# 64-row products in pairs, folds in two buffers and two parts, and rows 0 and 8 in halves, in a fused spectral and token-mixing kernel

## The chip, the cores and the metric

The kernel runs on 1 core of one Trainium2 chip. The metric is the device time in microseconds (us), the median of the runs shown. TensorE (PE) multiplies, VectorE (DVE) and ScalarE (ACT) work elementwise, SyncE (SP) issues nearly all DMAs; GpSimd (POOL) only sets four constants.

## The reference

x has 2048 rows (s) of 512 columns (d). Two branches are mixed by a gate that each row has:

```
g = sigmoid(sum_d(x * gate_w))
a = irfft2( rfft2(x) * (w_r + 1j * w_i) )             # over s (2048) and d (512)
h = layernorm(x) over d
u = gelu( h[s,d] * w1[s,f] summed over s + b1 )       # f: 1792
b = ( u[d,f] * w2[f,s] summed over f + b2 ), transposed to [s,d]
out = g * a + (1 - g) * b
```

Inputs and output are bfloat16; the normalisation has no weights.

## The kernel before

All of x is kept in SBUF. Its rows are taken as s = 512 q + 4 p + r: partition p (128), block q and residue r (4 each); row group j = 4q + r, 16 in all.

**The mixer** is two plain products on PE. The first (`m1`, L711 to L717) runs over the 14 column tiles `ft` of w1 and adds up 16 row groups in a bank of PSUM: product (ft, j) has 128 rows and 512 columns of the normalised x (`h`). Row groups are taken in the order 0, 8, 4, 12, and then residue by residue; for the first seven tiles each row group is multiplied for all seven before the next, so PE can begin as soon as group 0 is normalised. Gelu is on ACT (L732). The second (`m2`, L1022 to L1031) runs over the 16 row groups, with 14 products of 512 columns each in a bank; ACT evicts (L1034), DVE for the last two groups (L1041), of which the last is cut into 256, 128 and 128 columns.

**Normalisation.** DVE has a mean and variance (L489, L490; row 8 in two halves of 256, L505 and L507), ACT takes the root (L521), DVE the reciprocal (L526), and then DVE (L531, row groups 0, 8, 4, 1 and 12) or ACT (L537) writes `h`. Ahead of the first product PE multiplies ten times by a constant (L361).

**The spectral branch** is a transform over s in steps (radix 4 across q and r on DVE, dense products within), one over d (L664), the multiplication by the filter (L830 to L860), and then the inverse: radix 4 (L596 to L612), and the dense inverse products over s (L885 to L946). These are taken for each residue r (0 to 3), for each parity h of the columns and for lt = 0 and 1, the even and the odd wavenumbers. For odd r (`rs` = 1) the product at L903 has 128 rows of wavenumbers and 256 columns of a table; at lt = 0 the table holds a cosine (or sine) and the same with the sign turned for the upper 64 partitions, so that both s and its mirror come out. ACT evicts it to `zz` (L918); for even r it evicts to `ze` (L923), and DVE forms sum and difference (L933 to L937). DVE then adds lt = 0 and lt = 1 into z (`fq`, L943 and L944). The inverse over d (`i3`, L986 to L990) is taken for pairs of row groups p = 0 to 7, ACT evicts it with the gate (L994), and a fold on DVE (`es`, L1009 to L1013) forms the full row: a copy of two edge columns (L1009), a sum and a difference into the buffer `es`, and a sum and a difference back. L1047 adds the mixer's part, and SP stores.

**What sets the order.** Every step is a task with an engine, an estimated duration, what it reads and writes, a priority, and the buffers that it takes (`alloc`) and gives back (`free`). A planner (`Plan.order`, L173) runs these through a simulated clock and emits each engine's instructions in the order in which they were started. Each engine then runs its own list in that order; on PE the `m1` and `m2` products (late priority) are placed wherever no spectral product is ready. PSUM banks: four `acc`, two `fa`, two `fb`. The buffer `es` is there once (NES, L297).

Of the kernel before, what the change touches and what calls it, by code (L numbers as in the profile page):

```python
# [12 lines left out]
Alu = mybir.AluOpType  # L13
# [3 lines left out]
P = 128  # L17
# [227 lines left out]
def tt(n):  # L245
    return 0.07 + n / 1920.0
# [6 lines left out]
def d1(n):  # L253
    return 0.07 + n / 960.0
# [6 lines left out]
def mm(*ns):  # L261
    return sum(max(n, 62) / 2400.0 + 0.0025 for n in ns)
# [3 lines left out]
def tiny(k):  # L266
    return 0.09 * k + 0.06
# [3 lines left out]
def kernel(  # L271
# [22 lines left out]

    pool = ctx.enter_context(tc.tile_pool(name="sb", bufs=1))
    psum = ctx.enter_context(tc.tile_pool(name="ps", bufs=1, space=bass.MemoryType.PSUM))
    NES = 1  # L297

    def sb(shape, dt, tag, bufs=1):
        return pool.tile(shape, dt, tag=tag, name=tag, bufs=bufs)  # L300

    def ps(shape, dt, tag, bufs):
        return psum.tile(shape, dt, tag=tag, name=tag, bufs=bufs)
# [53 lines left out]
    def warm():  # L357
        pw = ps([P, D], F32, "fa", 2)
        zero = nc.const_aps.tensor(0.0, [P, 1], F32).bitcast(BF16)
        for _ in range(NWARM):  # L360
            T.matmul(pw[:], lhsT=zero[:, 0:1].to_broadcast([P, P]), rhs=zero[:, 0:1].to_broadcast([P, D]), start=True, stop=True)  # L361
# [107 lines left out]
    HACT = set(range(NJ)) - {0, 8, 4, 1, 12}  # L469
    PQ0 = -0.5  # L470
    ASTAT = {12, 4, 1}
    sqs = []
    rect = {}
    for r in range(4):
        xk = [("x", r, q) for q in range(4)]
        groups = [[q] for q in Q0] if r == 0 else [[0], [1], [2, 3]] if r == 1 else [[0, 1], [2], [3]] if 12 + r in ASTAT else [[0, 1], [2, 3]]
        t["xf", r] = None
        for b, qs in enumerate(groups):
# [8 lines left out]
            for j in js:  # L487
                def bn(j=j):
                    V.bn_stats(out=t["stats"][:, j, :], in_=t["x"][:, j // 4, j % 4, :])  # L489
                    V.bn_aggr(out=t["mv"][:, j, :], in_=t["stats"][:, j, :])  # L490
                def sum1(j=j):
                    xj, junk = t["x"][:, j // 4, j % 4, :], t["h"][:, j // 4, j % 4, :]
                    A.activation(junk, xj, ActF.Copy, scale=-1.0 / D, accum_out=t["mv"][:, j, 0:1])

                def sum2(j=j):
                    xj, junk = t["x"][:, j // 4, j % 4, :], t["h"][:, j // 4, j % 4, :]
                    A.activation(junk, xj, ActF.Square, bias=t["mv"][:, j, 0:1], scale=1.0, accum_out=t["mv"][:, j, 1:2])
                if j in ASTAT:
# [26 lines left out]
            def rec(colv=colv, mvv=mvv, js=js, here=here):  # L525
                V.reciprocal(colv("rstd"), colv("rstd"))  # L526
                if any(j in HACT for j in js):
                    V.scalar_tensor_tensor(colv("nmr"), mvv(0), 1.0 if here else -1.0, colv("rstd"), op0=Alu.mult, op1=Alu.mult)  # L528
                for j in js:
                    if j not in HACT:  # L530
                        V.tensor_scalar(t["h"][:, j // 4, j % 4, :], t["x"][:, j // 4, j % 4, :], t["mv"][:, j, 0:1],  # L531
                                        t["rstd"][:, j:j + 1], op0=Alu.add if j in ASTAT else Alu.subtract, op1=Alu.mult)
            own = [j for j in js if j not in HACT]
            rect[g] = add("DVE", 0.17 + 0.08 * (len(own) < len(js)) + 0.35 * len(own), rec, reads=xb + mvk, writes=[("rstd", *g)] + [("h", j) for j in own], prio=1.2 * r - (0.2 if r else 0.9))
# [170 lines left out]
    def w1of(ft):  # L705
        return sum(ft >= b for b in WB[1:3])
# [1 line left out]
    def bankof(ft):  # L708
        return "fa" if ft == 0 else "fb" if ft in (5, 6) else "acc"

    def m1(ft, j):  # L711
        if j == jorder[0]:
# [3 lines left out]
        T.matmul(t["u", ft][:], lhsT=w[:, j // 4, j % 4, c * P:(c + 1) * P],  # L716
                 rhs=t["h"][:, j // 4, j % 4, :], start=(j == jorder[0]), stop=(j == jorder[-1]))  # L717

    order = [(ft, j) for c in range(6) for j in jorder[2 * c:2 * c + 2] for ft in range(NF)]
    order += [(ft, j) for ft in range(NF) for j in jorder[12:]]  # L720
    order += [(ft, j) for ft in range(NF, NFT) for j in jorder]
# [4 lines left out]
    for n, (ft, j) in enumerate(order):  # L726
        last = j == jorder[-1]
        bank = bankof(ft)
        m1t.append(add("PE", mm(512), lambda ft=ft, j=j: m1(ft, j), reads=[("w1", w1of(ft), j), ("h", j)] + ([("w1", 0, j, n) for n in range(2)] if j % 4 == 0 else []), writes=[("u", ft)],
                       prio=10 + n * 1e-3, alloc=[bank] if j == jorder[0] else (), free={NF - 1: ["wa"], NF + 3: ["wb"], NFT - 1: ["wb"]}.get(ft, ()) if last else ()))  # L730
# [144 lines left out]
    for lt in range(2):  # L875
# [5 lines left out]
        if lt == 0:  # L881
            add("SP", 0.5, lambda: dma(t["B"][0:1, 0].rearrange("p e (c v) l -> p (e c) (v l)", c=2), t["s8"][P - 8:P]),
                reads=["s8"], writes=[("T", 0, 0), ("T", 0, 1)], prio=0, nbytes=8192)

    i1t = {}  # L885
    for rs, h in ((0, 0), (0, 1), (1, 0), (1, 1)):
        for r in (rs, rs + 2):
            for lt in range(2):
                tag = ("fa", "fb")[lt]

                def i1(h=h, r=r, lt=lt, tag=tag):
                    if "zz" not in t:
                        t["zz"] = sb([P, 2, 2, 2, 2, 2, 2, P], BF16, "X")
                        t["ze"] = sb([P, 2, 2, 2, 2, L], BF16, "h")
                    p1 = t["i1", h, r, lt] = ps([P, 2, L], F32, tag, 2)
                    o, w = ti_at(r)
                    ti = t["ti"][:, o:o + w]
                    for v in range(2):
                        d = lambda c: t["B"][:, lt, r, 2 * c + v, h:L:2]
                        if r % 2:  # L900
                            for c in range(2):
                                f = (2 * c if lt == 0 else 5 - c) * P
                                T.matmul(p1[:, v], lhsT=d(c), rhs=ti[:, f:f + L], start=(c == 0), stop=(c == 1))  # L903
                        else:
                            u = ti[:, 256 * lt:256 * lt + 256]
# [68 lines left out]
    for p in range(NJ // 2):  # L974
# [23 lines left out]
        def tb2j(j0=j0):  # L998
            tbuf(j0)
            return t["tb_"][:, j0:j0 + 3:2]  # L1000

        def es(p=p, j0=j0, late=late, tb2j=tb2j):
            e, s = eo_v(p), sb([P, 2, 2, 2, P], BF16, "es", NES)
            o = tb2j() if late else e
            if late:
                for i in range(2):
                    V.tensor_scalar_add(e[:, i, 0, 0:129], e[:, i, 0, 0:129], t["ombb2"][:, j0 + 2 * i:j0 + 2 * i + 1])
            o = o.rearrange("p j h (k d) -> p j (h k) d", k=2)
            V.tensor_copy(s[:, :, :, :, 0], e[:, :, :, 0:129:128].rearrange("p j h k -> p j k h"))  # L1009
            V.tensor_add(s[:, :, 0, :, 1:P], e[:, :, :, 1:P], e[:, :, :, P + 1:L])  # L1010
            V.tensor_sub(s[:, :, 1, :, P - 1:0:-1], e[:, :, :, 1:P], e[:, :, :, P + 1:L])
            V.tensor_add(o[:, :, 0:4:3], s[:, :, :, 0], s[:, :, :, 1])
            V.tensor_sub(o[:, :, 2:0:-1], s[:, :, :, 0], s[:, :, :, 1])  # L1013
        add("DVE", 0.2 + tiny(1) + 4 * tt(512) + (0.3 if late else 0), es, reads=(k1 + ["omg"]) if late else [],
            writes=ko if late else k1, prio=4, alloc=["es"], free=["es"], after=gates if late else ())

        for i, j in enumerate((j0, j1)):
            n = 2 * p + i
# [77 lines left out]
```

## Time and profile before

| | us |
|---|---|
| median of 3 runs | 126.31 (126.26 to 126.35) |
| the profiled execution | 126.59 |
| its span, first to last instruction | 124.8 |
| PE busy in the span | 121.2 |
| DVE busy | 113.4 |
| ACT busy | 82.6 |

The prediction quotes the profile of one execution. "Busy" is time in which an engine worked. The chain of work that ended last is followed back from the last instruction, at each step to what released it. A timeline row has a start, a length, an engine, a line, and what was written from what; in brackets stands idle time ahead of it and what ended that. L12 is line 12 of the kernel. A row of groups has the count behind an x, then the busy time, and the mean length of one in ns. Matmuls are pipelined: a row's length is from a product's start to the end of its last column, so neighbours overlap.

### The profile page before, as it was taken

How to read it: one execution, taken by the hardware profiler on the slowest of the kernel's cores; microseconds unless marked ns; L12 is line 12 of the kernel's file. 1: busy time of each engine (PE TensorE's matmuls, PEld its weight loads, DVE VectorE, ACT ScalarE, POOL GpSimd, SP SyncE). 2: the span in 40 equal slices, each digit the busy share in tenths (PEclk: the TensorE clock that was granted, in tenths of full speed). 3: DMA queues.
4: the chain of work that ended last, by engine and by line, in shares of the span. 5: the costliest groups of instructions: out<-in, count | busy, mean ns of one | idle time of the engine just before them, and what ended most of it. 6: DMA issues, size and time to landing. Idle time of an engine off the chain costs nothing.

```text
span 124.8 us, 2188 instructions
## 1 busy us (share of the span) xinstructions
PE 121.2 (97%) x773; PEld 68.8 (55%) x773; DVE 113.4 (91%) x274; ACT 82.6 (66%) x169; POOL 0.2 (0%) x4
## 2 busy tenths in 40 slices
PE   7999999999999999999999999999999999999990
PEld 2345655555655466744455555555578767655590
DVE  1889999999989999999999999999979999999961
ACT  3795889699999999999520003742289999952200
POOL 0000000000000000000000000000000000000000
PEclk9999999999999999999999999999999999999999
DMA  4998999994649936799999900000000000011751
GB/s 122 347 302 277 397 395 389 375 294 86 145 87 302 266 74 156 226 411 414 417 420 415 377 17 0 0 5 0 3 0 0 0 5 0 0 63 45 318 205 47
DMA packets 18202, 23.09 MB, mean 185 GB/s; under 512 B 2174, under 2 KB 15888, under 8 KB 18192
## 3 DMA queue, kind: packets, MB, share of 16 engines
q1 hardware_dynamic: 17616, 22.34, 52.6%
q10 hardware_dynamic: 576, 0.62, 1.6%
q8 instruction: 6, 0.10, 0.3%
q14 instruction: 4, 0.03, 0.1%
HBM read 20.84 MB, written 2.10 MB: 184 GB/s over the span
## 4 chain that ended last, share of the span: by engine, by line
PE 97%; DVE 0%; issue 0%
PE acc L1028 33%; PE acc L716 31%; PE fb L716 6%; PE fb L1028 5%; PE fa L361 4%; PE fa L716 3%; PE fa L664 1%; PE fb L664 1%; PE fa L903 1%; PE fa L566 1%; PE fb L903 1%; PE fa L565 1%; PE fb L990 1%; PE fa L990 1%; PE fa L568 1%; PE fa L567 1%
## 5 line engine op out<-in xcount | busy, mean ns | idle before, releaser
L716 PE MATMUL acc<-h,wb 128*128 128x512 bf16 x112 | 27.0, 379 | 0.0
L1028 PE MATMUL acc<-gl,wb 128*128 128x512 bf16 (+1 forms) x98 | 24.5, 372 | 0.0
L1028 PE MATMUL acc<-gl,wa 128*128 128x512 bf16 (+1 forms) x98 | 23.8, 372 | 0.0
L1034 ACT ACTIVATE x<-acc,ombb,omg 128x512 bf16<-128x512 f32 x12 | 9.1, 782 | 20.8 <-PE acc L1028 20.8
L1028 PEld LDWEIGHTS <-wa 128*128 128x128 bf16 x126 | 13.4, 113 | 9.9
L1028 PEld LDWEIGHTS <-wb 128*128 128x128 bf16 x126 | 13.3, 114 | 9.2
L716 PE MATMUL acc<-h,wa 128*128 128x512 bf16 x64 | 17.4, 385 | 0.0
L716 PEld LDWEIGHTS <-wb 128*128 128x128 bf16 x112 | 10.7, 98 | 10.3
L716 PEld LDWEIGHTS <-wa 128*128 128x128 bf16 x112 | 10.4, 99 | 10.5 <-issue 0.7
L571 ACT CAST xp<-fa 128x512 bf16<-128x512 f32 x16 | 9.1, 584 | 2.4 <-PE fa L568 2.3
L746 ACT ACTIVATE x<-x 128x512 bf16<-128x512 bf16 x16 | 10.0, 649 | 0.0
L716 PE MATMUL fb<-h,wa 128*128 128x512 bf16 x32 | 9.9, 379 | 0.0
L489 DVE BATCH_NORM_STATS2 stats<-x 128x6 f32<-128x512 bf16 x12 | 8.1, 676 | 1.9 <-DMA x<-in_A_x_dram 1.9
L732 ACT ACTIVATE gl<-acc,b1f 128x512 bf16<-128x512 f32 x11 | 7.7, 701 | 2.8 <-PE acc L716 2.8
L537 ACT ACTIVATE h<-x,nmr,rstd 128x512 bf16<-128x512 bf16 x11 | 8.4, 808 | 1.1 <-DVE nmr L528 1.1
L716 PE MATMUL fa<-h,wa 128*128 128x512 bf16 x16 | 6.3, 392 | 0.0
L664 PEld LDWEIGHTS <-X 128*128 128x128 bf16 x64 | 4.7, 98 | 2.2
L994 ACT ACTIVATE B<-fa,g 128x512 bf16<-128x512 f32 x8 | 5.8, 727 | 0.0
L994 ACT ACTIVATE B<-fb,g 128x512 bf16<-128x512 f32 x8 | 5.8, 719 | 0.0
L361 PE MATMUL fa<-const-float32-0.0 128*128 128x512 bf16 x10 | 4.4, 629 | 0.8 <-PEq L1080 0.8
L671 ACT CAST X<-fb 128x512 bf16<-128x512 f32 x8 | 5.1, 638 | 0.0
L671 ACT CAST X<-fa 128x512 bf16<-128x512 f32 x8 | 5.1, 634 | 0.0
(176 smaller groups left out, 235.9 us busy)
## 6 DMA issues: line engine op xcount, KB each, us to landing
wb<-in_B_w_dram SPq DMA_DIRECT2D x11, 512.0 KB
wa<-in_B_w_dram SPq DMA_DIRECT2D x7, 512.0 KB
wa<-in_B_w_dram SPq DMA_DIRECT2D x2, 896.0 KB
wb<-in_B_w_dram SPq DMA_DIRECT2D x4, 384.0 KB
out_dram<-x SPq DMA_DIRECT2D x3, 512.0 KB
x<-in_A_x_dram SPq DMA_DIRECT2D x2, 512.0 KB
wa<-in_B_w_dram SPq DMA_DIRECT2D x4, 224.0 KB
rot<-dft_ti SPq DMA_DIRECT2D x1, 768.0 KB
```

Source lines behind the costliest of these rows:

```text
L361: T.matmul(pw[:], lhsT=zero[:, 0:1].to_broadcast([P, P]), rhs=zero[:, 0:1].to_broadcast([P, D]), start=True, stop=True)
L489: V.bn_stats(out=t["stats"][:, j, :], in_=t["x"][:, j // 4, j % 4, :])
L537: add("ACT", 0.71, lambda j=j: A.activation(t["h"][:, j // 4, j % 4, :], t["x"][:, j // 4, j % 4, :], ActF.Identity, bias=t["nmr"][:, j:j ...
L571: add("ACT", act(512), lambda r=r, dq=dq: A.copy(xe(r)[:, :, :, dq, :], t["pa", r, dq][:]), reads=[("pa", r, dq)], writes=[("X", r, dq)], ...
L664: T.matmul(pb[:, k % 2, k // 2], lhsT=t["X"][:, lt, EX[e], c, k, :], rhs=tbl(k, c), start=True, stop=True)
L671: A.copy(t["X"][:, lt, EX[e]].rearrange("p c j l -> p (c j l)").rearrange("p (h c g b) -> p h c g b", h=2, c=2, b=2)[:, :, c], t["pb", lt, ...
L716: T.matmul(t["u", ft][:], lhsT=w[:, j // 4, j % 4, c * P:(c + 1) * P], rhs=t["h"][:, j // 4, j % 4, :], start=(j == jorder[0]), stop=(j == ...
L732: gelus.append(add("ACT", act(512, 1) , lambda ft=ft: A.activation(t["gl"][:, ft, :], t["u", ft][:], ActF.Gelu_apprx_tanh, bias=t["b1f"][: ...
L746: A.activation(t["x"][:, q, r, :], t["x"][:, q, r, :], ActF.Copy, accum_out=t["glog"][:, 4 * q + r:4 * q + r + 1])
L994: A.activation(eo_v(p)[:, n].rearrange("p h (n w) -> p h n w", w=2), t["i3", j][:].rearrange("p h (w n) -> p h n w", w=2), ActF.Copy, scal ...
L1028: T.matmul(t["y", j, m][:, cs], lhsT=w[:, o, 512 * q + r:512 * q + 512:4], rhs=t["gl"][:, ft, cs], start=(ft == 0), stop=(ft == NFT - 1))
L1034: A.activation(tbuf(j).rearrange("p h d -> p (h d)"), t["y", j, 0][:], ActF.Identity, bias=t["ombb2"][:, j:j + 1], scale=t["omg"][:, j:j + 1])
```

## The change

1. **Odd residues, lt = 0.** For each h one task `i1s` takes the place of two `i1` tasks (r = 1 and 3). It makes products of 64 rows and 128 columns: the lower 64 partitions into a bank `fa`, the upper 64 into a bank `fb`, each adding c = 0 and 1, for two residues and two v: 16 products per h. The table's sign-turned copy isn't read any more: ACT copies the two banks to a new tile `zo` (in the buffer `h`, behind `ze`), and DVE forms their sum and difference into `zz` (`eo2`).
2. **The banks of lt = 1** for odd r: `fa` for r = 1 and `fb` for r = 3 (all `fb` before).
3. **Folds.** `es` has two buffers. The fold is two tasks, `es` and `es2`, the second with the earlier priority (3.95, against 4). For seven of eight folds ACT copies the edge (`ese`), not DVE.
4. **Rows 0 and 8.** `nrm` normalises 256 columns; the second half is a task of its own. The products of these rows in the first seven tiles are of 256 columns each, all seven tiles with the first half, then all seven with the second. For row 8 the aggregation of the statistics is its own task.
5. **Warm-up.** Nine products of 512 columns and one of 256, in place of ten of 512.

```diff
-    NES = 1
+    NES = 2
...
-        for _ in range(NWARM):
-            T.matmul(pw[:], lhsT=zero[:, 0:1].to_broadcast([P, P]), rhs=zero[:, 0:1].to_broadcast([P, D]), start=True, stop=True)
-    NWARM = 10
-    add("PE", 0.42 * NWARM, warm, writes=["warmed"], prio=-5, alloc=["fa"], free=["fa"])
+        for n in [D] * 9 + [L]:
+            T.matmul(pw[:, 0:n], lhsT=zero[:, 0:1].to_broadcast([P, P]), rhs=zero[:, 0:1].to_broadcast([P, n]), start=True, stop=True)
+    add("PE", 4.0, warm, writes=["warmed"], prio=-5, alloc=["fa"], free=["fa"])
...
+    HALF = (0, 8)
...
+    def nrm(j, n):
+        c = slice(L * n, L * n + L)
+        V.tensor_scalar(t["h"][:, j // 4, j % 4, c], t["x"][:, j // 4, j % 4, c], t["mv"][:, j, 0:1], t["rstd"][:, j:j + 1], op0=Alu.subtract, op1=Alu.mult)
...
-                            if n:
-                                V.bn_aggr(out=t["mv"][:, 8, :], in_=t["st8"][:].rearrange("p n s -> p (n s)"))
-                        add("DVE", d1(L) + 0.2 * n, bnh, reads=[("x", 0, 2)], writes=[("mv", 8)], prio=-0.6 - 0.5 * n, after=[rect[0, 0]] if n else ())
+                        add("DVE", d1(L), bnh, reads=[("x", 0, 2)], writes=[("mv", 8)], prio=-0.6 - 0.6 * n, after=[rect[0, 0]] if n else ())
+                    add("DVE", 0.13, lambda: V.bn_aggr(out=t["mv"][:, 8, :], in_=t["st8"][:].rearrange("p n s -> p (n s)")), writes=[("mv", 8)], prio=-1.2)
...
                 for j in js:
-                    if j not in HACT:
+                    if j in HALF:
+                        nrm(j, 0)
+                    elif j not in HACT:
...
+            if js[0] in HALF:
+                j = js[0]
+                add("DVE", 0.2, lambda j=j: nrm(j, 1), reads=xb + [("rstd", *g)], writes=[("h", j, 1)], prio=-1.1)
...
-    order = [(ft, j) for c in range(6) for j in jorder[2 * c:2 * c + 2] for ft in range(NF)]
+    order = [(ft, j, n) for j in jorder[:12] for n in ((0, 1) if j in HALF else (None,)) for ft in range(NF)]
...
+    MMR = 8 * mm(128) + 0.1
     i1t = {}
     for rs, h in ((0, 0), (0, 1), (1, 0), (1, 1)):
+        if rs:
+            def i1s(h=h):
+                p2 = t["i1s", h] = [ps([P, 2, 2, P], F32, tag, 2) for tag in ("fa", "fb")]
+                for n, r in enumerate((1, 3)):
+                    ti = t["ti"][:, ti_at(r)[0]:]
+                    for v in range(2):
+                        for c in range(2):
+                            for m in range(2):
+                                k = slice(64 * m, 64 * m + 64)
+                                T.matmul(p2[m][:, n, v], lhsT=t["B"][k, 0, r, 2 * c + v, h:L:2], rhs=ti[k, 2 * c * P:2 * c * P + P], start=(c == 0), stop=(c == 1))
+            i1t[h, 1, 0] = i1t[h, 3, 0] = add("PE", MMR, i1s, reads=[("T", 0, 1), "ti"], writes=[("i1s", h)], prio=3, alloc=["fa", "fb"])
+            for m in range(2):
+                add("ACT", act(512), lambda h=h, m=m: A.copy(t["zo"][:, h, m], t["i1s", h][m][:]), reads=[("i1s", h)] + pbk, writes=[("zo", h, m)],
+                    prio=1.7, free=[("fa", "fb")[m]], after=[lined])
+
+            def eo2(h=h):
+                for k, f in enumerate((V.tensor_add, V.tensor_sub)):
+                    f(t["zz"][:, 1, h, 0, :, k].rearrange("p v r a -> p r v a"), t["zo"][:, h, 0], t["zo"][:, h, 1])
+            add("DVE", 2 * tt(512), eo2, reads=[("zo", h, m) for m in range(2)], writes=[("zz", h, r, 0) for r in (1, 3)], prio=3.55)
         for r in (rs, rs + 2):
-            for lt in range(2):
-                tag = ("fa", "fb")[lt]
+            for lt in range(rs, 2):
+                tag = ("fa", "fb")[lt if not rs else r // 2]
...
+        if not late:
+            def ese(p=p):
+                t["es", p] = sb([P, 2, 2, 2, P], BF16, "es", NES)
+                edge(A.copy, t["es", p], eo_v(p))
+            add("ACT", 0.22, ese, reads=[("eo", j0), ("eo", j1)], writes=[("es", p)], prio=1.4, alloc=["es"])
...
+        def es2(p=p):
+            s, o = t["es", p]
             V.tensor_add(o[:, :, 0:4:3], s[:, :, :, 0], s[:, :, :, 1])
             V.tensor_sub(o[:, :, 2:0:-1], s[:, :, :, 0], s[:, :, :, 1])
...
+        add("DVE", (0.15 if late else 0.02) + 2 * tt(512) + (0.3 if late else 0), es, reads=(k1 + ["omg"]) if late else [("es", p)],
+            writes=[("es", p)] + (ko if late else k1), prio=4, alloc=["es"] if late else [], after=gates if late else ())
+        add("DVE", 2 * tt(512), es2, reads=[("es", p)], writes=ko if late else k1, prio=3.95, free=["es"])
```

More of the change, by code (lines that the diff above doesn't have):

```diff
@@ L533 @@
             own = [j for j in js if j not in HACT]
-            rect[g] = add("DVE", 0.17 + 0.08 * (len(own) < len(js)) + 0.35 * len(own), rec, reads=xb + mvk, writes=[("rstd", *g)] + [("h", j) for j in own], prio=1.2 * r - (0.2 if r else 0.9))
+            rect[g] = add("DVE", 0.17 + 0.08 * (len(own) < len(js)) + 0.35 * len(own) - 0.15 * (js[0] in HALF), rec, reads=xb + mvk, writes=[("rstd", *g)] + [("h", j) for j in own], prio=1.2 * r - (0.2 if r else 0.9))
+            if js[0] in HALF:
+                j = js[0]
+                add("DVE", 0.2, lambda j=j: nrm(j, 1), reads=xb + [("rstd", *g)], writes=[("h", j, 1)], prio=-1.1)
             for j in js:
@@ L709, in bankof, with m1 @@
         return "fa" if ft == 0 else "fb" if ft in (5, 6) else "acc"
-    def m1(ft, j):
-        if j == jorder[0]:
+    def m1(ft, j, n):
+        if j == jorder[0] and not n:
             t["u", ft] = ps([P, D], F32, bankof(ft), NB[bankof(ft)])
@@ L715, in m1 @@
         w, c = t["wa"] if k == 0 else t["wb", k - 1], ft - WB[k]
-        T.matmul(t["u", ft][:], lhsT=w[:, j // 4, j % 4, c * P:(c + 1) * P],
-                 rhs=t["h"][:, j // 4, j % 4, :], start=(j == jorder[0]), stop=(j == jorder[-1]))
-    order = [(ft, j) for c in range(6) for j in jorder[2 * c:2 * c + 2] for ft in range(NF)]
-    order += [(ft, j) for ft in range(NF) for j in jorder[12:]]
-    order += [(ft, j) for ft in range(NF, NFT) for j in jorder]
+        d = slice(0, D) if n is None else slice(L * n, L * n + L)
+        T.matmul(t["u", ft][:, d], lhsT=w[:, j // 4, j % 4, c * P:(c + 1) * P],
+                 rhs=t["h"][:, j // 4, j % 4, d], start=(j == jorder[0] and not n), stop=(j == jorder[-1]))
+    order = [(ft, j, n) for j in jorder[:12] for n in ((0, 1) if j in HALF else (None,)) for ft in range(NF)]
+    order += [(ft, j, None) for ft in range(NF) for j in jorder[12:]]
+    order += [(ft, j, n) for ft in range(NF, NFT) for j in jorder for n in (None,)]
     add("ACT", 1.6, lambda: A.activation(t["ombb2"][:, 0:1], t["rstd"][:, 0:1], ActF.Gelu_apprx_tanh),
@@ L725 @@
     m1t = []
-    for n, (ft, j) in enumerate(order):
+    for n, (ft, j, half) in enumerate(order):
         last = j == jorder[-1]
         bank = bankof(ft)
-        m1t.append(add("PE", mm(512), lambda ft=ft, j=j: m1(ft, j), reads=[("w1", w1of(ft), j), ("h", j)] + ([("w1", 0, j, n) for n in range(2)] if j % 4 == 0 else []), writes=[("u", ft)],
-                       prio=10 + n * 1e-3, alloc=[bank] if j == jorder[0] else (), free={NF - 1: ["wa"], NF + 3: ["wb"], NFT - 1: ["wb"]}.get(ft, ()) if last else ()))
+        m1t.append(add("PE", mm(512 if half is None else L), lambda ft=ft, j=j, half=half: m1(ft, j, half), reads=[("w1", w1of(ft), j), ("h", j)] + ([("h", j, 1)] if half != 0 and j in HALF else []) + ([("w1", 0, j, n) for n in range(2)] if j % 4 == 0 else []), writes=[("u", ft)],
+                       prio=10 + n * 1e-3, alloc=[bank] if j == jorder[0] and not half else (), free={NF - 1: ["wa"], NF + 3: ["wb"], NFT - 1: ["wb"]}.get(ft, ()) if last else ()))
         if last:
@@ L893, in i1 @@
                         t["zz"] = sb([P, 2, 2, 2, 2, 2, 2, P], BF16, "X")
-                        t["ze"] = sb([P, 2, 2, 2, 2, L], BF16, "h")
+                        hb = sb([P, 8192], BF16, "h")
+                        t["ze"] = hb[:, 0:4096].rearrange("p (h r i v n) -> p h r i v n", h=2, r=2, i=2, v=2)
+                        t["zo"] = hb[:, 4096:6144].rearrange("p (h m r v n) -> p h m r v n", h=2, m=2, r=2, v=2)
                     p1 = t["i1", h, r, lt] = ps([P, 2, L], F32, tag, 2)
@@ L901, in i1 @@
                             for c in range(2):
-                                f = (2 * c if lt == 0 else 5 - c) * P
+                                f = (5 - c) * P
                                 T.matmul(p1[:, v], lhsT=d(c), rhs=ti[:, f:f + L], start=(c == 0), stop=(c == 1))
@@ L1000, in tb2j, with edge @@
             return t["tb_"][:, j0:j0 + 3:2]
+        def edge(f, s, e):
+            f(s[:, :, :, :, 0], e[:, :, :, 0:129:128].rearrange("p j h k -> p j k h"))
+        if not late:
[3 more added lines that the diff above has]
+            add("ACT", 0.22, ese, reads=[("eo", j0), ("eo", j1)], writes=[("es", p)], prio=1.4, alloc=["es"])
         def es(p=p, j0=j0, late=late, tb2j=tb2j):
-            e, s = eo_v(p), sb([P, 2, 2, 2, P], BF16, "es", NES)
+            e, s = eo_v(p), sb([P, 2, 2, 2, P], BF16, "es", NES) if late else t["es", p]
             o = tb2j() if late else e
@@ L1008, in es @@
             o = o.rearrange("p j h (k d) -> p j (h k) d", k=2)
-            V.tensor_copy(s[:, :, :, :, 0], e[:, :, :, 0:129:128].rearrange("p j h k -> p j k h"))
+            if late:
+                edge(V.tensor_copy, s, e)
             V.tensor_add(s[:, :, 0, :, 1:P], e[:, :, :, 1:P], e[:, :, :, P + 1:L])
             V.tensor_sub(s[:, :, 1, :, P - 1:0:-1], e[:, :, :, 1:P], e[:, :, :, P + 1:L])
+            t["es", p] = s, o
+        def es2(p=p):
+            s, o = t["es", p]
             V.tensor_add(o[:, :, 0:4:3], s[:, :, :, 0], s[:, :, :, 1])
             V.tensor_sub(o[:, :, 2:0:-1], s[:, :, :, 0], s[:, :, :, 1])
-        add("DVE", 0.2 + tiny(1) + 4 * tt(512) + (0.3 if late else 0), es, reads=(k1 + ["omg"]) if late else [],
-            writes=ko if late else k1, prio=4, alloc=["es"], free=["es"], after=gates if late else ())
+        add("DVE", (0.15 if late else 0.02) + 2 * tt(512) + (0.3 if late else 0), es, reads=(k1 + ["omg"]) if late else [("es", p)],
+            writes=[("es", p)] + (ko if late else k1), prio=4, alloc=["es"] if late else [], after=gates if late else ())
+        add("DVE", 2 * tt(512), es2, reads=[("es", p)], writes=ko if late else k1, prio=3.95, free=["es"])
         for i, j in enumerate((j0, j1)):
```

## The prediction

> **What bounds the kernel now.** I read first the page's busy shares and its chain of work that ended last, then the stretches (busy time of each engine between two moments), then the chain in order of time, and last the timeline around the edited steps.
>
> ```profile
> PE 121.2 (97%) x773; PEld 68.8 (55%) x773; DVE 113.4 (91%) x274; ACT 82.6 (66%) x169; POOL 0.2 (0%) x4
> ...
> PE 97%; DVE 0%; issue 0%
> ```
>
> The chain is TensorE (PE) from end to end. A busy share can hide short stalls, so the stretches come next. Their columns are the stretch, its length, and the busy time of PE, weight load, DVE, ACT and POOL.
>
> ```profile
> 5.20:38.40 33.20, 33.20 (x194) 17.49 (x193) 31.20 (x95) 28.94 (x62) 0.00 (x0) 1.00 0.88 279
> ...
> 90.50:99.10 8.60, 8.60 (x85) 6.62 (x84) 7.61 (x20) 8.20 (x17) 0.00 (x0) 1.00 0.00 0
> 99.10:109.00 9.90, 9.90 (x109) 7.05 (x108) 9.35 (x26) 9.87 (x18) 0.00 (x0) 1.00 0.01 2
> 109.00:122.00 13.00, 12.95 (x88) 8.20 (x86) 11.26 (x32) 3.58 (x6) 0.00 (x0) 1.00 0.41 157
> ```
>
> PE has no idle time between 5.20 and 109. DVE and ACT are nearly full in single stretches, ACT most of all from 90.5 to 109, but PE doesn't wait for them, as its order is filled up with products of the token mixer. The chain in order of time (start, length, what) gives the price of one product:
>
> ```profile
> 0.77 4.43 PE fa L361 x10
> 5.20 0.43 PE fa L716
> 5.62 1.15 PE acc L716 x4
> ...
> 35.17 3.24 PE acc L716 x15
> ...
> 93.34 0.06 PE fb L911
> ...
> 93.99 0.44 PE fa L903 x4
> ```
>
> A 512-column product takes 3.24/15 = 0.216 us, a 256-column one 0.44/4 = 0.11, a 128-column one 0.06 (of which 0.056 is by proportion: 0.216 x 128/512 = 0.054, and a bit for the issue). They follow each other at that spacing with weights changed each time, so PE streams without a gap, and the time of the kernel is the sum of the columns that PE streams, a start and a tail. An edit is worth what it takes from this sum; what it does on DVE and ACT counts only where it makes PE wait, or outlasts PE at the end.
>
> **The change part by part.**
>
> *1. The products of the odd residues.* Removed are, for each half h and residue 1 and 3, the four 256-column products at lt = 0 (L903): 2 x 2 x 4 = 16, or 16 x 0.11 = 1.75 us (by 0.109 each). Added are, for each h, sixteen 128-column products with 64 rows each: 32 in 16 pairs, the two of a pair on the lower and the upper 64 partitions and into different banks. No 64-row product is in this trace, so I bound the pair from both sides: 0.056 us if its two products run side by side, 0.112 if one follows the other. 16 pairs are 0.90 or 1.79 us. What the weight loads need is shown: each product brings its own, and the narrowest products follow each other every 0.03 us with a load each:
>
> ```profile
> 99.30 0.03 PE fa L987
> 99.33 0.03 PE fa L988
> 99.36 0.11 PE fa L990 x2
> ```
>
> Two loads and two products in 0.06 us are thus a rate that this kernel reaches already. Nothing in the issue forbids the overlap, and the two halves share neither rows nor bank; I take 0.056 a pair, which gives -0.85 us. The other end is +0.04 us.
>
> The Trainium skill, "TensorE: Matmul & The Clock Gate", Part 3 (Packing small matmuls), says that products in different row groups run at the same time, each further one starting some 4 ns later; as an estimate 16 pairs would be 16 x (0.056 + 0.004) = 0.96 us, a gain of 0.79; no run here shows it yet.
>
> *2. Going into the 64-row form and back.* The sixteen products of one h are a block between full-height ones, so there are four changes of form. The trace has none. The lower end is nothing: at 93.34 the array goes from 512-column products to 128-column ones of another source and bank at full spacing. The upper end is the array's depth, where the form may change only when it is empty:
>
> ```profile
> L903 PE MATMUL fa<-rot,B 128*128 128x256 bf16 x16 | 2.4, 273 | 0.0
> ...
> L911 PE MATMUL fb<-rot,B 128*128 128x128 bf16 x8 | 1.2, 218 | 0.0
> ```
>
> A 128-column product lasts 218 ns though the next starts after 55: 0.16 us from its last column to its end. Four times that is 0.65 us. I take 0.07 a change, 0.28 in all: under half of the depth, as the nearer row is that of the change that costs nothing, and not zero, as something has to part the two forms.
>
> The Trainium skill, "TensorEngine Tiling (Array Packing)", Key Properties, says that a change of the tiling mode (not of the tile) drains TensorE; it names no price. With a full drain the sum is that of the second rival below.
>
> *3. Start.* The warm-up loses half a product, 0.21 us at the early spacing of 0.43. Below are the nearest narrow normalisation, in the groups by line, and the first rows of the timeline:
>
> ```profile
> L1007 DVE TENSOR_SCALAR B<-B,ombb 128x129 bf16<-128x129 bf16 x2 | 0.4, 256 | 0.0
> ```
>
> ```profile
> 4.37 0.16 DVE L526 RECIPROCAL rstd<-rstd 128x1 f32<-128x1 f32 x1
> 4.57 0.41 DVE L531 TENSOR_SCALAR h<-x,mv,rstd 128x512 bf16<-128x512 bf16 x1
> ...
> 4.85 0.29 PEld L716 LDWEIGHTS <-wa 128*128 128x128 bf16 x2 [0.56 <-DMA wa<-in_B_w_dram]
> ...
> 5.03 0.59 PE L716 MATMUL fa<-h,wa 128*128 128x512 bf16 x1
> ...
> 6.12 0.41 DVE L531 TENSOR_SCALAR h<-x,mv,rstd 128x512 bf16<-128x512 bf16 x1
> ...
> 7.04 0.38 PE L716 MATMUL fa<-h,wa 128*128 128x512 bf16 x1
> ```
>
> Row 0 is normalised at 4.98 and its first product starts at 5.03; the warm-up ends in the chain at 5.20, and the array takes the next product 0.17 before that, 5.03 too: both limits stand at one place, so each edit alone would bring nothing. A half row takes between 0.26 (129 columns) and 0.41 (512); with 0.33 the half is ready at 4.90 and PE starts at 4.95 (the weights were there at 4.85). That is 0.08 us earlier, but in the slow part: the chain shows products of 0.43 us until about 6.2 (four in 1.15 us are 1.4 slow and 2.6 fast). If the fast rate comes at the same time as before, 0.08 us at half rate is worth 0.04. The ends are 0 (PE waits for something else) and 0.11 (all of the 0.21 at half rate). The second half of row 0 has seven slow half products, 1.5 us, to arrive in. Row 8 is ready at 6.53 for a product at 7.04: 0.5 us of cover, so its halving is worth nothing; were that cover gone, each 0.1 us of lateness would be 0.1 us.
>
> The 14 products of the two rows become 28 of half width: 2 x 0.109 - 0.216 = 0.002 to 0.004 us each, +0.04. The additional DVE instructions (two halves in place of one, twice, some 0.15 us each) lie in the stretch from 5.20 to 38.40, where DVE idles 2.0 us.
>
> *4. DVE and ACT behind it.* ACT's evictions stay four of 512 columns per h. DVE gets a sum and a difference of 512 per h, and loses the small edge copy of seven of eight folds, which ACT takes.
>
> ```profile
> 111.23 0.42 DVE L1012 TENSOR_TENSOR B<-es 128x512 bf16<-128x512 bf16 x1
> 111.57 0.42 DVE L1013 TENSOR_TENSOR B<-es 128x512 bf16<-128x512 bf16 x1
> ...
> 112.10 0.19 DVE L1009 COPY es<-B 128x8 bf16<-128x8 bf16 x1
> 112.18 0.42 DVE L1010 TENSOR_TENSOR es<-B 128x508 bf16<-128x508 bf16 x1
> ...
> 112.51 0.42 DVE L1011 TENSOR_TENSOR es<-B 128x508 bf16<-128x508 bf16 x1
> ...
> 113.04 0.43 DVE L1012 TENSOR_TENSOR B<-es 128x512 bf16<-128x512 bf16 x1
> ```
>
> Starts tell the cost: 0.34 us for a 512-wide operation (111.23 to 111.57), 0.08 for the edge copy (112.10 to 112.18), and 0.53 where the next needs the result (112.51 to 113.04) or the one buffer (111.57 to 112.10): 0.19 of waiting. So +4 x 0.34 = +1.36, -7 x 0.08 = -0.56, and the two buffers and the fold in two parts can hide up to 0.19 in each of seven folds and the three places where two folds adjoin: -1.9 at most. Together DVE is between +0.8 and -1.1 us; I take -0.2. The sum and difference come ahead of the z of the odd residues, whose first use has cover:
>
> ```profile
> 100.50 0.69 DVE L944 TENSOR_TENSOR xp<-X 128x1024 bf16<-128x1024 bf16 x1
> ...
> 104.13 0.25 PE L986 MATMUL fa<-tg,xp 128*128 128x191 bf16 x1
> ```
>
> z is complete at 101.19, and the first of its products (the fifth pair) starts at 104.13: 2.9 us, against 1.4 of delay. ACT gets seven edge copies; the nearest small operation costs 0.2 to 0.3:
>
> ```profile
> 10.20 0.48 ACT L521 ACTIVATE rstd<-mv,eps 128x1 f32<-128x1 f32 x2
> ```
>
> Two in 0.48 us make 0.2 each by spacing: 1.4 us on an ACT that idles 0.03 in its stretch. Behind them wait the evictions of the next fold and thus the banks of the next L990 block. Its lateness runs into the time from 109 on, where ACT is busy 3.58 of 13; it costs PE nothing as long as the order of PE has mixer products in front of each block. Its price if not is the third rival below.
>
> *5. Tail.*
>
> ```profile
> 119.08 0.74 DVE L1041 SCALAR_TENSOR_TENSOR x<-acc,omg,x 128x512 bf16<-128x512 f32 x1
> ...
> 120.43 0.48 DVE L1041 SCALAR_TENSOR_TENSOR x<-acc,omg,x 128x256 bf16<-128x256 f32 x1 [0.60 <-PE acc L1028]
> ...
> 121.21 0.35 DVE L1041 SCALAR_TENSOR_TENSOR x<-fa,omg,x 128x128 bf16<-128x128 f32 x1 [0.29 <-PE fa L1028]
> ...
> 121.99 0.35 DVE L1041 SCALAR_TENSOR_TENSOR x<-fb,omg,x 128x128 bf16<-128x128 f32 x1 [0.43 <-PE fb L1028]
> ```
>
> DVE waits 0.60 + 0.29 + 0.43 = 1.3 us for PE here. PE that ends 0.6 earlier leaves 0.7, and even DVE's worst end (+0.8) would pass that by 0.1 only. The last operation and its store move with PE. No DMA is added or taken out, and SyncE's queue keeps its loads.
>
> **Sum:** -0.85 + 0.28 - 0.04 + 0.04 = -0.57 us. The profiled execution took 126.59 (span 124.8 and 1.8 around it); it becomes 126.02. The median of the runs is 0.28 lower, 126.31, and becomes 125.74, say 125.7.
>
> **The rivals.**
>
> *Pairs in turn* (the other side; also the case that the pairs aren't pairs). The two products of a pair follow each other: +0.04, and the four changes of form cost 0.28 to 0.65, with no gain to pay for them: +0.3 to +0.7, 126.6 to 127.0. It decides from 0.092 us a pair on (16 pairs and 0.28 then equal 1.75). For it: no row shows two products at once. Against it: rows and banks are apart.
>
> *Full drain at each change.* The overlap is there, -0.85, but 4 x 0.16 = 0.65 goes back: -0.2, 126.1. For it: the depth in the L911 row.
>
> *ACT late for PE's banks.* From 99 on ACT has 1.4 us more work and no idle time; if the order of PE counts on less, each of the six later blocks waits some 0.1 us: 0.6 us, and the time is 126.3. For it: ACT 9.87 of 9.90. Against it: 13 us of mixer products still to be placed. A new order elsewhere that makes PE wait has the same look.
>
> **How the numbers follow.** My forecast (125.3 to 126.0) gets 0.55, pairs in turn 0.17, full drain 0.14, ACT late 0.14. A measurement of this kernel can tell about 0.2%, 0.25 us, from no change. Forecast: faster. Full drain lies at the bound: half faster, half same. ACT late: half same, 0.03 faster, 0.04 slower. That makes faster 0.65, same 0.14, slower 0.21. The range leaves out the worse part of pairs in turn: 125.2 (no cost of the changes of form, the start's best end: 126.31 - 0.85 - 0.11 - 0 + 0.04, and 0.15 for scatter of the terms) to 126.7.
>
> **What would show it.** Step 1: in the chain the sixteen products of one h take about 0.45 us, 0.9 if in turn. Step 2: a gap ahead of and behind each block, 0.16 with a full drain. Step 3: the first L716 product near 4.95, the fast rate at the same time as now. Step 4: no wait of PE in the stretch from 99 to 109, DVE's last wide L1041 before about 120. Step 5: DVE still waits for PE at the end. The prediction fails if PE shows idle time inside the span, or if the pairs don't overlap.

## The result, and the profile after

The changed kernel takes 125.98 us (median of 14 runs, 125.89 to 126.95), the kernel before 126.35 (14 runs, 126.26 to 126.77). The ratio is 0.9973, with a 95% interval of 0.9961 to 0.9984: 0.34 us faster, between 0.20 and 0.49. The profiled execution took 126.27 us with a span of 124.5. The page's first lines, and the stretches that were shown of before:

```profile
span 124.5 us, 2256 instructions
...
PE 120.7 (97%) x803; PEld 69.2 (56%) x803; DVE 113.5 (91%) x273; ACT 83.8 (67%) x176; POOL 0.2 (0%) x4
```

```profile
5.20:38.40 33.20, 33.14 (x207) 18.68 (x206) 31.47 (x97) 28.98 (x60) 0.00 (x0) 1.00 0.87 278
...
90.50:99.10 8.60, 8.60 (x102) 6.04 (x101) 7.60 (x21) 8.13 (x17) 0.00 (x0) 1.00 0.01 2
99.10:109.00 9.90, 9.90 (x101) 6.79 (x100) 9.73 (x26) 9.59 (x21) 0.00 (x0) 1.00 0.00 0
109.00:122.00 13.00, 12.61 (x94) 8.25 (x92) 11.22 (x30) 4.97 (x10) 0.00 (x0) 1.00 0.42 158
```

PE still has no idle time from 90.5 to 109, DVE and ACT are as full as they were, and what is missing of PE's work shows in the last stretch, where PE ends earlier. The chain in order of time has one block of the new products (start, length, what):

```profile
96.44 0.43 PE acc L1075 x2
96.88 0.16 PE fa L907
97.03 0.00 PE fb L907
97.04 0.05 PE fa L907
...
97.43 0.00 PE fb L907
97.43 0.56 PE acc L1075 x2
```

The upper product of a pair (bank `fb`) costs 0.00, the lower 0.05: the pairs run side by side, 0.055 us each. The first one takes 0.16, 0.10 too much, and the two full products behind the block 0.56 in place of 0.43, 0.13 too much. A block thus takes 0.55 + 0.13 = 0.68 us (96.88 to 97.43, and the delay behind it); the eight products that it replaces took 0.87.

The starts of executions differ (more on that below), so I measure from the first product with the second part of w1 to PE's end. In before (the profile of the kernel before) that is 35.01 to 121.97, in after (that of the changed kernel) 35.05 to 121.62. First the lines of before, then those of after:

```profile
35.01 1.24 PE L716 MATMUL acc<-h,wb 128*128 128x512 bf16 x5
```

```profile
121.17 0.80 PE fb L1028 x14
121.97 0.03 issue
```

```profile
35.05 1.24 PE L726 MATMUL acc<-h,wb 128*128 128x512 bf16 x5
```

```profile
120.83 0.80 PE fb L1075 x14
121.62 0.03 issue
121.65 0.35 DVE x L1088
```

86.96 us before, 86.57 after: 0.39 less, which is 2 x (0.87 - 0.68) within 0.01. The whole gain of PE is there. Up to 35 us nothing was won: 35.01 and 35.05.

### The profile page after: what moved, and what is told of

Read it like the earlier page. It is cut to its first block, busy times and chain, and to the rows that moved or that the text cites. A ratio compares the mean times of both kernels' runs of the same rounds, so it can differ in the third digit from the quotient of the medians.

```text
span 124.5 us, 2256 instructions
## 1 busy us (share of the span) xinstructions
PE 120.7 (97%) x803; PEld 69.2 (56%) x803; DVE 113.5 (91%) x273; ACT 83.8 (67%) x176; POOL 0.2 (0%) x4
## 4 chain that ended last, share of the span: by engine, by line
PE 79%; DMA 11%; SPq 6%; ACTq 1%; issue 1%; DVE 0%
PE acc L1075 33%; PE acc L726 24%; DMA b1b<-in_B_b_dram 7%; SPq L312 6%; PE fb L1075 5%; DMA wa<-in_B_w_dram 4%; PE fb L726 2%; PE fa L673 1%; PE fb L673 1%; PE fa L726 1%; PE fa L907 1%; PE fa L574 1%; PE fa L575 1%; PE fb L1022 1%; PE fa L1022 1%; PE fa L935 1%
## 5 line engine op out<-in xcount | busy, mean ns | idle before, releaser
L1075 PEld LDWEIGHTS <-wa 128*128 128x128 bf16 x126 | 13.4, 113 | 9.6
L726 PE MATMUL acc<-h,wa 128*128 128x512 bf16 (+1 forms) x72 | 17.5, 356 | 0.0
L726 PEld LDWEIGHTS <-wa 128*128 128x128 bf16 x126 | 11.7, 98 | 8.9 <-issue 0.5
L726 PE MATMUL fb<-h,wa 128*128 128x512 bf16 (+1 forms) x36 | 10.3, 355 | 0.0
L726 PE MATMUL fa<-h,wa 128*128 128x512 bf16 (+1 forms) x18 | 6.5, 360 | 0.1
L361 PE MATMUL fa<-const-float32-0.0 128*128 128x512 bf16 (+1 forms) x10 | 4.2, 608 | 0.8 <-PEq L1127 0.8
```

Source lines behind the costliest of these rows:

```text
L726: T.matmul(t["u", ft][:, d], lhsT=w[:, j // 4, j % 4, c * P:(c + 1) * P], rhs=t["h"][:, j // 4, j % 4, d], start=(j == jorder[0] and not n ...
L1075: T.matmul(t["y", j, m][:, cs], lhsT=w[:, o, 512 * q + r:512 * q + 512:4], rhs=t["gl"][:, ft, cs], start=(ft == 0), stop=(ft == NFT - 1))
```

## The experiments

Theory P: the pairs carry the gain, 0.87 us less streaming minus four changes of form (0.46), and the rest of the change nets nothing. Theory R: the start and the folds carry it, and the pairs give back what they save. Each run was timed beside the kernel before; the third column is the stretch of PE from the first product with the second part of w1 to its last, from the run's profile. A median differs by up to 0.2 us from one comparison to the next (the kernel before has 126.35 to 126.57), so ratios are compared, and of two ratios only what exceeds their intervals, some 0.2 us each way, counts as shown.

| run | ratio to before (95%) | PE from w1's second part on, us |
|---|---|---|
| before | 1 | 86.96 |
| after | 0.9973 (0.9961 to 0.9984) | 86.57 |
| after_2 | 0.9983 (0.9966 to 1.0000) | 86.57 |
| pairs_only | 1.0076 (1.0055 to 1.0097) | 86.56 |
| no_pairs | 1.0008 (0.9992 to 1.0024) | 86.96 |
| pairs_folds | 0.9969 (0.9950 to 0.9988) | 86.57 |
| in_turn | 1.0017 (1.0002 to 1.0033) | 87.05 |
| split_blocks | 1.0024 (1.0004 to 1.0043) | 87.11 |
| one_block | 0.9952 (0.9933 to 0.9970) | 86.34 |
| one_block_2 | 0.9979 (0.9961 to 0.9997) | 86.34 |
| bias_late | 1.0720 (1.0684 to 1.0756) | - |
| bias_moved | 1.0106 (1.0084 to 1.0128) | - |
| both | 1.0690 (1.0656 to 1.0724) | - |
| block_moved | 1.0094 (1.0071 to 1.0116) | - |

**pairs_only.** The kernel before with points 1 and 2 of the change; one buffer, whole folds, the old start:

```diff
 NES = 1
+        if rs:
+            def i1s(h=h):
...
-            for lt in range(2):
+            for lt in range(rs, 2):
```

> The kernel before with the 64-row pairs alone. Theory P (the pairs carry the gain: 16 pairs take 0.054 us each, and going into and out of the 64-row form costs 0.10 and 0.13 us, as the trace of after shows; the rest of the change nets nothing): 0.41 us under the kernel before, 125.9. VectorE has 1.36 us more to do without the doubled folds; its cover at the end is 1.3 us, of which 0.4 goes, so up to 0.4 of the gain can be lost there (126.3 at worst, with VectorE and not PE last at the end). Theory R (the start and the folds carry the gain, and the pairs give back in changes of form what they save): no change, 126.35.

Measured 127.44 against 126.57: 0.87 us slower by the medians, 0.96 by the ratio. Both theories missed it. PE did its part, 0.4 us less (86.56), and ends at 121.53; but the kernel doesn't get faster. The timeline of the end:

```profile
120.04 0.68 DVE L1069 TENSOR_TENSOR x<-x,B 128x1024 bf16<-128x1024 bf16 x1
120.64 1.14 DVE L1063 SCALAR_TENSOR_TENSOR x<-acc,omg,x 128x512 bf16<-128x512 f32 x2
...
121.41 1.49 SPq L312 DMA_DIRECT2D out_dram<-x  x3
121.69 0.34 DVE L1063 SCALAR_TENSOR_TENSOR x<-fa,omg,x 128x128 bf16<-128x128 f32 x1
121.95 0.34 DVE L1063 SCALAR_TENSOR_TENSOR x<-fb,omg,x 128x128 bf16<-128x128 f32 x1
122.32 0.35 ACTq L312 DMA_DIRECT2D out_dram<-x  x1
```

```profile
122.00:123.00 1.00, 0.00 (x0) 0.00 (x0) 0.29 (x2) 0.00 (x0) 0.00 (x0) 1.00 0.96 373
```

The second is its stretch from 122 to 123, where the last two columns are the DMA share and GB/s. In before the same work lay earlier: the last 1024-wide addition, the issue of the late stores behind it, and the stretches from 120 to 123:

```profile
118.48 0.68 DVE L1047 TENSOR_TENSOR x<-x,B 128x1024 bf16<-128x1024 bf16 x1
119.19 0.99 SPq L312 DMA_DIRECT2D out_dram<-x  x2
```

```profile
120.00:122.00 2.00, 1.95 (x32) 1.79 (x30) 0.85 (x3) 0.00 (x0) 0.00 (x0) 1.00 0.95 354
122.00:123.00 1.00, 0.00 (x0) 0.00 (x0) 0.34 (x1) 0.00 (x0) 0.00 (x0) 1.00 0.20 45
```

In pairs_only DVE no longer waits for PE: its last 1024-wide addition begins at 120.04, in before at 118.48, 1.56 later. The last DVE operation ends when it did in before (122.3), but the span is 0.9 us longer: the stores of the late rows are issued at 120.75 and 121.41, in before at 119.19 and 119.85, and the bulk of them moves behind 122 us, with the DMA engines 96% busy, with the last small stores among it. So work on DVE that ends when PE does still costs here, by the stores behind it. This is read from the two traces; no run moves the stores alone.

**no_pairs.** The changed kernel without points 1 and 2.

```diff
-        if rs:
-            def i1s(h=h):
...
-            for lt in range(rs, 2):
+            for lt in range(2):
```

> The changed kernel without the 64-row pairs: halves, warm-up and folds stay. Theory P: as the kernel before within 0.1 us, 126.3, with waits of PE for loads between 15 and 23 us of the span (0.15 and 0.2 us) that eat what the start gains. Theory R: as the changed kernel, 126.0.

1.0008: as the kernel before, and PE's stretch is 86.96 again. R has fallen: start and folds by themselves bring nothing. The waits that theory P names aren't in this trace, though: its products became fast later than in after (four half products still take 1.06 us from 5.44 on), so PE comes late to both places (the second part of w1 starts at 35.48) and finds the row and the bias there.

**pairs_folds.** The changed kernel with the old start: ten products of warm-up, rows 0 and 8 whole.

```diff
-        for n in [D] * 9 + [L]:
+        for _ in range(NWARM):
...
-    HALF = (0, 8)
```

> The kernel before with the pairs and the folds (two buffers, two parts, edges on ScalarE), but its own start: ten products of warm-up, rows 0 and 8 whole. Theory now: TensorE gets 0.41 us shorter by the pairs, and the folds take VectorE's added work out of the end, where it held up the stores in the run with pairs alone; the start adds nothing, because PE has to wait for a normalised row at 15.7 and for the bias at 22.7 us in any case. It then takes as long as the changed kernel, 0.3% under the kernel before, within 0.1 us. Rival: the start has a share; then it is 0.1 to 0.35 us slower than the changed kernel.

0.9969, against 0.9973 for the changed kernel: level, within the intervals of some 0.2 us. Together with pairs_only that settles who does what: the pairs shorten PE, the folds make room on DVE without which the pairs cost 0.9 us, and the start does nothing that shows. No run takes the three parts of the folds (two buffers, two tasks, edges on ACT) apart, nor the pairs and the banks of point 2. How the folds make room is in the timeline of DVE in after:

```profile
102.76 0.42 DVE L1052 TENSOR_TENSOR es<-B 128x508 bf16<-128x508 bf16 x1
103.10 0.42 DVE L1053 TENSOR_TENSOR es<-B 128x508 bf16<-128x508 bf16 x1
103.43 0.42 DVE L1052 TENSOR_TENSOR es<-B 128x508 bf16<-128x508 bf16 x1
103.77 0.42 DVE L1053 TENSOR_TENSOR es<-B 128x508 bf16<-128x508 bf16 x1
104.11 0.41 DVE L1058 TENSOR_TENSOR B<-es 128x512 bf16<-128x512 bf16 x1
...
117.64 0.68 DVE L1094 TENSOR_TENSOR x<-x,B 128x1024 bf16<-128x1024 bf16 x1
```

Two folds alternate, everything follows at 0.33 or 0.34 us, and the waits of 0.19 of before are gone. DVE's last addition begins at 117.64, 0.84 earlier than before, in spite of 1.36 us of additional work (0.56 us of edge copies went to ACT).

**in_turn.** The same products, first the eight on the lower 64 partitions, then the eight on the upper:

```diff
-                for n, r in enumerate((1, 3)):
-                    ...
-                            for m in range(2):
+                for m in range(2):
+                    for n, r in enumerate((1, 3)):
```

> The changed kernel with the sixteen products of one h in another order: first the eight on the lower 64 partitions, then the eight on the upper. If the overlap comes from neighbours in the order that sit on different halves, it is gone: 32 products of 0.054 us in place of 16 pairs, 0.87 us more, 126.8 to 126.9. If TensorE finds the overlap by itself however they are ordered: no change, 126.0.

0.48 us more in PE's stretch, not 0.87. The order decides, but not fully; the timeline of one block shows why:

```profile
96.97 0.45 PE L907 MATMUL fa<-rot,B 64*128 64x128 bf16 x5
97.21 0.23 PE L907 MATMUL fb<-rot,B 64*128 64x128 bf16 x1
97.25 0.22 PE L907 MATMUL fa<-rot,B 64*128 64x128 bf16 x1
97.28 0.22 PE L907 MATMUL fb<-rot,B 64*128 64x128 bf16 x1
97.31 0.21 PE L907 MATMUL fa<-rot,B 64*128 64x128 bf16 x1
97.33 0.22 PE L907 MATMUL fb<-rot,B 64*128 64x128 bf16 x1
97.37 0.22 PE L907 MATMUL fa<-rot,B 64*128 64x128 bf16 x1
97.39 0.44 PE L907 MATMUL fb<-rot,B 64*128 64x128 bf16 x5
```

The first product of the upper half starts at 97.21, ahead of three of the lower half that stand before it in the program. So, by the recorded starts, three of the eight pairs still overlap: TensorE starts products of the other half a few places ahead. With neighbours on different halves all of them overlap.

**split_blocks.** One full product of 128 columns in the middle of each block (its result is overwritten by the next ones):

```diff
+                    if n:
+                        T.matmul(p2[0][:, 1, 1], lhsT=t["B"][:, 0, 1, 0, h:L:2], rhs=ti[:, 0:P], start=True, stop=True)
```

> The changed kernel with one full-height product of 128 columns put into the middle of each block of sixteen (its result is overwritten by the next 64-row products): four more changes of form, nothing else. If a change costs 0.10 going in and 0.13 coming out, wherever it lies: 2 x 0.23 + 2 x 0.054 = 0.57 us more than the changed kernel, 126.55. If the edges of a block cost only because of what stands around it (loads of the mixer products, banks): 0.1 us more.

0.54 us more in PE's stretch; by the ratios, of two comparisons, 0.0051 or 0.64 us. The chain has it at the place:

```profile
96.99 0.00 PE fb L909
97.00 0.16 PE fa L904
97.16 0.16 PE fa L909
```

The full product takes 0.16 and the first pair behind it 0.16, 0.054 being due to each: 0.11 us a change, four more of them and the two products, 0.54. A change of form costs 0.10 to 0.13 in all of these places, so the mixer's products around a block aren't the cause. What in the change takes the time isn't told apart by these runs: at each of them the load of the first weights of the new form begins only with the first product (in after at 96.80 for a product at 96.81), where the loads inside a block start some 0.05 us ahead of theirs.

**one_block** and **one_block_2**. All 32 products in one task that takes all four banks (the planner counts how many a task takes of a kind):

```diff
-        if rs:
-            def i1s(h=h):
+        if rs and not h:
+            def i1s():
+                for h in range(2):
...
-... all(caps[a] > 0 for a in t.alloc)
+... all(caps[a] >= t.alloc.count(a) for a in t.alloc)
```

> The changed kernel with the products of both h in one block of 32, which takes all four banks at once: two changes of form in place of four. Theory P: 0.10 + 0.13 = 0.23 us less, 125.75, if PE has other products to do until the four banks are free. If the cost at the edges of a block belongs to the pairs (the first pair of a bank) and not to the change of form, or if the wait for the banks eats it: no change or slower, 126.0 or more.

> The one block of 32 again: 0.23 us (0.2%) under the changed kernel of the same call, if two changes of form less are what it won; level with it, if the first comparison was chance.

PE's stretch is 86.34 in both, 0.23 under the changed kernel, as expected. The whole time says less: 0.9952 the first time (the changed kernel, in another comparison, 0.9973), 0.9979 the second, beside 0.9983 for the changed kernel on the same chip (after_2; the medians are 126.23 and 126.25 us). It beats the kernel before in both. That it beats the changed kernel in whole time isn't shown: side by side the two were level, and the start of an execution, below, varies by more than the 0.23 us.

> The changed kernel once more, beside the next three on one chip: 0.3% under the kernel before.

That run came out at 0.9983, within the interval of the first comparison; its own interval reaches 1.0000.

**bias_late** and **both**. In after PE waits at the product that turns the bias; the priority was to bring it later.

```diff
-    ... writes=["pbias"], prio=-1, alloc=["fa"])
+    ... writes=["pbias"], prio=10.085, alloc=["fa"])
```

> The changed kernel with the small product that turns the bias placed later in PE's order, past the time at which its load lands. If that load holds PE: the wait of 0.2 us at 22.7 us is gone, and 0.2 us are won, 125.8, or nothing, if the next thing that PE waits for takes its place (the loads of the second part of w1 near 35 us). Rival: the wait is an artefact of one execution: no change, 126.0, without a new wait.

> One block of 32 and the bias late together: if both count, 0.23 + 0.2 = 0.43 us under the changed kernel, 125.55. If only the block counts: 125.75.

9 us slower, both. In the planner's order the product came behind the spectral products that take the same bank `fa`; it ran at 40.0 us, and ACT's gelus, which need the bias, had to come after it. Below are the product, and the stretch in which it ran:

```profile
L705 PE MATMUL fa<-flip,b1b x1: 173/173/173, 40.0 to 40.0; 128*128 128x14 bf16 x1
```

```profile
38.40:53.70 15.30, 12.10 (x70) 6.09 (x70) 12.16 (x31) 12.69 (x30) 0.00 (x0) 0.69 0.78 230
```

PE idled for 3.2 us of this stretch and its granted clock fell to 0.69. The two runs say nothing on what the bias's wait costs.

**bias_moved** and **block_moved**. The same product, moved by seven tasks in the finished order, all else as it was:

```diff
     order_ = pl.order()
+    k = order_.index(bt)
...
+    order_[k:k] = [bt, bv]
```

> The changed kernel with the bias product moved by seven tasks in PE's finished order, after its load has landed, and nothing else in the order changed. If the wait at 22.7 us is what keeps the start's lead from the end: up to 0.2 us less than the changed kernel. If the next wait takes its place, or if the wait is there in some executions alone: no change.

> One block and the moved bias product: 0.23 us under the changed kernel by the block, and up to 0.2 more by the bias; 0.23 alone if the bias holds nothing.

Slower by 1.1 and 0.9%. The product now stood behind a spectral block that had taken the second `fa` bank, and waited for ACT to empty it:

```profile
26.14 0.17 PE L705 MATMUL fa<-flip,b1b 128*128 128x14 bf16 x1 [1.40 <-ACT xp L580]
```

Another wait, and a longer one, took the place of the one removed. So none of these four runs tells what the bias's wait costs; the traces of the others do, as the next section shows.

## Why the prediction was right, point by point

It said 0.57 us less; it was 0.34, with the sign as said, and the place and the mechanism of the products too. One term was mis-sized, and two others came out for reasons that it didn't give.

*1. The products.* Right: 16 pairs at 0.055, 0.87 against 0.85. The Trainium skill ("TensorE: Matmul & The Clock Gate", Part 3) says that products in different row groups run at the same time. The trace agrees: the second of a pair starts within 0.01 us of the first.

*2. The changes of form.* This is the term that was mis-sized: 0.07 each was taken, 4 x 0.07 = 0.28, and the trace has 0.10 going in and 0.13 coming out, 0.46 for the four. split_blocks (four more: +0.54 with its two products) and one_block (two fewer: -0.23) confirm it. With it the sum would have been -0.39. The Trainium skill ("TensorEngine Tiling (Array Packing)", Key Properties) says that a change of the tiling mode drains TensorE. These gaps agree in that every change costs, but at 0.10 to 0.13 us they stay short of the 0.16 that the prediction took for the full depth. The value was between my row that cost nothing and the full depth of 0.16; I had leaned to the wrong one, since a change of shape is not a change of form.

*3. The start.* -0.04 and +0.04, and indeed nothing (pairs_folds), but that it fits is in part luck. The half row came at 5.03 in the profiled execution, not at 4.90: the first statistics started at 3.21 in place of 3.09, as x landed later. PE's first product came at 5.08, not near 4.95, and the fast spacing didn't come at the same time as before: in after it is there from 5.24 us on, in before from about 6.2. So in after PE was 0.33 us ahead at 14.82 (the product that started at 15.15 in before); at 35 it was level. The lead went in two waits:

```profile
15.15 0.59 PE L726 MATMUL fb<-h,wa 128*128 128x512 bf16 x2
15.73 0.38 PE L726 MATMUL fa<-h,wa 128*128 128x512 bf16 x1
...
22.33 0.38 PE L726 MATMUL fb<-h,wa 128*128 128x512 bf16 x1
22.77 0.18 PE L705 MATMUL fa<-flip,b1b 128*128 128x14 bf16 x1
```

The first is 0.58 where two products need 0.43: ACT is normalising that row just then (two rows in 1.52 us from 14.87 on). The second is 0.44 where one product needs 0.22, and the view of waits names the load of the bias:

```profile
PEld L705 <- DMA b1b<-in_B_b_dram: 0.6, 1, 0.6
```

Here one sign by which the prediction would fail did show, if small: 0.06 us of PE's 33.20 from 5.20 to 38.40 are idle, at 22.71, just ahead of this product. The other traces confirm that nothing else takes time up to 35 us. In all ten of the table with a stretch it is 12.24 or 12.25 us from the product behind the bias to the first with w1's second part. split_blocks has the same order as after up to there, and in its execution the bias was there in time:

```profile
22.35 0.38 PE L726 MATMUL fb<-h,wa 128*128 128x512 bf16 x1
22.57 0.17 PE L705 MATMUL fa<-flip,b1b 128*128 128x14 bf16 x1
```

Its second part starts at 34.84, 0.21 earlier than in after, and one_block's, without the wait too, at 34.82; after_2 has the wait and starts at 35.07. So the bias's wait costs PE 0.2 us where it occurs, and it occurs in some executions alone.

*4. DVE and ACT.* DVE came out 0.84 us earlier, within the bounds (+0.8 to -1.1) and nearer their better end than the -0.2 that I took. ACT's edge copies cost nothing on the path; the third rival didn't come.

*5. Tail.* Right for this change, as the folds kept DVE early, but the price given for the bad end was wrong: "even DVE's worst end (+0.8) would pass that by 0.1 only" leaves out the stores. In pairs_only DVE is 1.56 us later, and the kernel 0.9 us slower with PE 0.4 earlier: I had counted how long DVE's last operations wait for PE, and not the large stores, which go out only when DVE's last additions are done.

*Rivals.* Pairs in turn: not so (in_turn, which puts the halves one after the other, costs 0.48, and not 0.87, as three pairs of eight still overlap). Full drain: half true, at 0.115 in place of 0.16.

## What to carry to other kernels

Where one engine is full from end to end, count its streaming alone, and price every change of its mode: here 64-row pairs save 0.054 us each, and a block must hold more than four of them before its two edges (0.23 us) are paid; so put them in as few blocks as the banks allow. A saving on the full engine can be lost if the work that it moves lands on the second-fullest one: undo the relief (here the folds, without which 0.4 us less of PE became 0.9 us more) and see. The end can be set by stores too, so look at when the last large ones are issued, not only at the last instruction.

## What the runs showed of the hardware

Two products of 64 rows on different halves of the partitions, into different banks, overlap fully (0.055 us a pair), and by the recorded starts TensorE even starts one ahead of three others that precede it in the program (97.21, against 97.25 to 97.37, in in_turn).

The time at which products become fast differs between executions of one kernel (here on two chips): in one_block the half products follow at 0.11 us from 5.18 on, in one_block_2 four of them still take 1.06 from 5.29:

```profile
5.18 0.60 PE L726 MATMUL acc<-h,wa 128*128 128x256 bf16 x4
```

```profile
5.29 1.06 PE L726 MATMUL acc<-h,wa 128*128 128x256 bf16 x4
```

The Trainium skill ("TensorE: Matmul & The Clock Gate", Part 1) has it that the clock's window runs freely and doesn't begin with the kernel. That would make this time differ as it does here; the profile doesn't show it, as the granted clock reads 1.00 from the start in both. The difference is still 0.43 us at 35 us (34.82 and 35.25), more than the change itself won, and the two executions took 125.78 and 126.22 us. So the medians need many runs; a stretch behind the start came out the same to 0.01 us in both profiles of the changed kernel, and of one_block, and tells small edits on PE apart.
